# Seven block products in place of eight for the in-projection of a second MoE, in groups of two weight tiles

## The chip, the cores and the metric

One core of a Trainium2 chip. The metric is the device time of one execution in microseconds (us); before: median 705.96 of 3 runs (705.52 to 706.01). Engines are named TensorE (PE; its weight loads PEld), VectorE (DVE), ScalarE (ACT), GpSimd (POOL) and SyncE (SP, which issues DMAs here).

## What is computed

Three stages in sequence, in fp32 from float64 inputs (two 32-bit words per value): bucketed attention, a first MoE, a second MoE. B = 2, H = 8, S = 768, D = 64, so 1536 tokens of 512 values.

```python
scores = where(q_bucket == k_bucket, (q @ k.T) / sqrt(D), -1e9)
x = softmax(scores) @ v                                  # 1536 x 512
h = maximum(maximum(x @ w1, x @ w2), x @ w3)             # 512 -> 768
x = h @ w_out                                            # 768 -> 512
h = x @ m2_in                                            # 512 -> 2048
g = h / (1 + exp(-1.702 * h))
out = g @ m2_out                                         # 2048 -> 512
```

## The kernel before

Precision: TensorE multiplies in fp32r. Every operand is held as a high part (a copy rounded to fp32r, by ScalarE) and a low part (value minus high part, by GpSimd or VectorE), and every product is three matmuls: high x high, high x low, low x high.

Attention (L307 to L403): for each head and each 128 queries, `scores` (L307) makes a 128x768 tile in PSUM by four matmuls of 384 columns (two halves of the keys, each in its own bank, two contraction pieces), `clamp` (L319) brings it to SBUF with a minimum on VectorE, then Exp on ScalarE, scaling on GpSimd, transposes on TensorE (L346), the split into high and low (L352, L356) and the product with v (L364). A planner (`plan`, L47) with costs and due times (`COST`, `DUE`) fixes the order of all these tasks.

First MoE: `up1` (L554) for 6 feature tiles x 3 matrices x 3 token chunks of 512 (12 matmuls each, L561), `split1` (L576), `down1` (L584; 18 matmuls each, L594), whose result is X[1], the second MoE's input, as high and low parts `xh`, `xl` (128 x 4 x 1536).

Second MoE: 16 feature tiles (FT2) in 4 groups of 4 (FG = 4). `up2(f, a)` (L605) takes the 128 features f of chunk a: 4 contraction blocks x 3 matmuls = 12 matmuls of 512 columns (L612) into one PSUM bank, then sigmoid on ScalarE (L620), product on VectorE (L621), high part gh on ScalarE (L622), low part gl on GpSimd (L623). `down2(k, t)` (L625) takes 128 tokens: 4 tiles x 3 matmuls (L633) into one bank; group 0 copies it to `res` (L639, ScalarE), later groups add it (L641, VectorE), the last one stores it (L644). The loop at L870 runs the ups of one group and chunk, then the downs of the chunk before it.

Weights: each 128x512 block comes raw by DMA (512 KB; `w_load`, L436, two buffers WRAW) and is turned into fp32 by `w_steps` (L449): Abs on ScalarE (L456), clamp on GpSimd (L460), three VectorE steps of shift (L468), low word (L472) and sign (L476), after which the raw buffer is free and the next load is issued, then high part on ScalarE (L483) and low part on GpSimd (L496). Split tiles lie in rings of 6 ("w" for in-projections, "wo" for out-projections; WBUFS).

Order: each engine runs its instructions in the order of the program (`in_order`, L647). In the MoEs `unit` (L846) issues one up or down and then calls `w_tick` (L510), which moves each weight block in flight on by one step; a new block starts when enough matmuls have been issued (PACE, `owed`), at most three at once, and a block's split waits (and all behind it) until a buffer of its ring is free by program order (`w_free`, L504). PSUM in the MoEs is a ring of 8 banks (`bank`, L547).

Of the kernel before, what the change touches and what calls it, by code (L numbers as in the profile page):

```python
# [5 lines left out]
F32 = mybir.dt.float32  # L6
# [7 lines left out]
P = 128  # L14
# [76 lines left out]
def build(tc, q, k, v, proj, w1, w2, w3, w_out, m2_in, m2_out, out):  # L91
# [41 lines left out]

    def f32(ap):
        return ap.bitcast(F32)

    def halves(ap):
        return ap.rearrange("p (a n) -> p a n", a=2)

    def psum_halves(ap):  # L140
        return ap.rearrange("p (a n) -> p a n", a=2)[:, :, :HALF]


    warm = st([P, 512], "warm", 1, BF16)
# [162 lines left out]
    def scores(u):  # L307
        hd, c = divmod(u, NTILE)
        ks, qs = stacks[hd]
        pss = ps_s()  # L310
        for a in range(2):
            nc.tensor.matmul(pss[:, a * 512:a * 512 + HALF], qs[:, 0, c * P:(c + 1) * P],  # L312
                             ks[:, 0, a * HALF:(a + 1) * HALF], start=True, stop=False)
        for a in range(2):
            nc.tensor.matmul(pss[:, a * 512:a * 512 + HALF], qs[:D + NA, 1, c * P:(c + 1) * P],  # L315
                             ks[:D + NA, 1, a * HALF:(a + 1) * HALF], start=False, stop=True)
# [108 lines left out]
    for n in range(FT2 // FG):  # L425
        for f in range(n * FG, (n + 1) * FG):
            w_block(("in", f), m2_in[:, f * P:(f + 1) * P].rearrange("(c p) f -> p c f", p=P), EC, "w")
        if n > 0:
            w_out_group(n)
    WIDE = w1.dtype == U64  # L430
    WRAW = 2
    WBUFS = {"w": 6, "wo": 6}
    wraw, wsplit = {}, {}
    wstate = [0, 0]

    def w_load():  # L436
        i = wstate[0]
# [64 lines left out]
    wflight = []  # L502

    def w_free(i):  # L504

# [1 line left out]
        mine = [j for j in range(i) if wblocks[j][2] == tag]  # L507
        return len(mine) < WBUFS[tag] or mine[-WBUFS[tag]] in wdone

    def w_tick(start):  # L510
# [9 lines left out]
        if start and i < len(wblocks) and len(wflight) < 3 and (mo[0] is not None or wblocks[i][2] == "w"):  # L520
# [28 lines left out]
        return mo[1].tile([P, CH], F32, tag="acc", name=f"acc_{seq[0]}", bufs=8)  # L549

    def hm_tile():
        return st([P, CH], "hm", 4, pool=mo[0]) if mo[0] else st([P, CH], "hm0", 1)

    def up1(ft, i, a, get, later=False):  # L554
        wh, wl = w_get("up", ft, i)
# [49 lines left out]
    def up2(f, a):  # L605
        xh, xl = X[1]
        wh, wl = w_get("in", f)
        s = slice(a * CH, (a + 1) * CH)
        o = bank()
        for c in range(EC):  # L610
            for z, (w, x) in enumerate(((wh, xh), (wh, xl), (wl, xh))):
                nc.tensor.matmul(o, w[:, c, :], x[:, c, s], start=(c == 0 and z == 0),  # L612
                                 stop=(c == EC - 1 and z == 2))
        if a == NCH - 1:
            wdone.add(wplace["in", f])
        gh = st([P, CH], "gh", 2 * FG + 1, F32R, mo[2])
        gl = st([P, CH], "gl", 2 * FG + 1, F32R, mo[2])
        gs[f, a] = (gh, gl)
        g = hm_tile()
        nc.scalar.activation(g, o, AF.Sigmoid, scale=1.702)  # L620
        nc.vector.tensor_tensor(out=g, in0=o, in1=g, op=ALU.mult)  # L621
        nc.scalar.copy(gh, g)  # L622
        nc.gpsimd.tensor_tensor(out=gl, in0=g, in1=f32(gh), op=ALU.subtract)  # L623

    def down2(k, t):  # L625
        a, j = divmod(t, CH // P)
        s = slice(j * P, (j + 1) * P)
        ws = [w_get("out", k * FG + n) for n in range(FG)]
        o = bank()
        for n in range(FG):  # L630
            (gh, gl), (wh, wl) = gs[k * FG + n, a], ws[n]
            for z, (g, w) in enumerate(((gh, wh), (gh, wl), (gl, wh))):
                nc.tensor.matmul(o, g[:, s], w.rearrange("p c f -> p (c f)"),  # L633
                                 start=(n == 0 and z == 0), stop=(n == FG - 1 and z == 2))
        if t == B * NTILE - 1:
            wdone.update(wplace["out", k * FG + n] for n in range(FG))
        if k == 0:
            res[t] = st([P, E], "res", B * NTILE, F32, mo[2])
            nc.scalar.copy(res[t], o)  # L639
        else:  # L640
            nc.vector.tensor_tensor(out=res[t], in0=o, in1=res[t], op=ALU.add)  # L641
        if k == FT2 // FG - 1:
            b, c = divmod(t, NTILE)
            nc.sync.dma_start(out[b * S:(b + 1) * S, :].rearrange("(p c) e -> c p e", c=NTILE)[c], res[t])  # L644


    def in_order(first):  # L647
# [8 lines left out]
    if True:  # L656
# [186 lines left out]
        split1(0, 0)  # L843
        owed = [2 * PACE]

        def unit(fn, *args, after=None, matmuls=12):  # L846
            fn(*args)
            if after:
                after()
            owed[0] = min(owed[0] + matmuls / 12, 2 * PACE)  # L850
            for _ in range(1 if matmuls == 12 else 2):
                if w_tick(owed[0] >= PACE):
                    owed[0] -= PACE

        for a in range(1, NCH):
# [12 lines left out]
        NK = FT2 // FG  # L868
        ups = [(m, a) for m in range(NK) for a in range(NCH)]
        for n in range(len(ups) + 2):  # L870
            if n < len(ups):
                m, a = ups[n]
                for f in range(m * FG, (m + 1) * FG):
                    unit(up2, f, a)
            if n > 0 and n - 1 < len(ups):
                m, a = ups[n - 1]
                for t in range(a * CH // P, (a + 1) * CH // P):
                    unit(down2, m, t)
        in_order(first)
        sb_g.__exit__(None, None, None)  # L880
        ps_toe.__exit__(None, None, None)
# [31 lines left out]
```

## Time and profile before

| | us |
|---|---|
| median of 3 runs | 705.96 (705.52 to 706.01) |
| the profiled execution | 706.35 |
| its span, first to last instruction | 704.5 |
| attention, up to the first MoE's matmuls in one run | 0 to 251.2 |
| first MoE | 251.2 to 438.9 |
| second MoE | 438.9 to 704.5 |

In the table the stages are told by the first and last matmul of their lines. Rows of the trace give an engine, a line of the kernel, an operation with the tiles it writes and reads, and times in us unless ns is said. Matmul records overlap, as matmuls are pipelined, so the time of one is read from a block's length and count, not from its record.

### The profile page before, as it was taken

To read this page: it belongs to the slowest core of one execution; us is meant where nothing else is said; L and a number is where in the kernel's file an instruction comes from. 1 tells how busy PE (TensorE), PEld (TensorE's weight loads), DVE (VectorE), ACT (ScalarE), POOL (GpSimd) and SP (SyncE) were. 2 spreads that over 40 slices of the span, in tenths; PEclk is the share of its full clock that TensorE was granted. 3 is DMA by queue.
4 is the path that set the end of the run, shared out by engine and by line. 5 is a ranking of instruction groups with operands and counts; after the bars stand their busy time and mean duration, and the time that the engine had idled before them with its cause. 6 is when DMAs were issued, how large, how long until landed. Compare 5 with 4: busy or idle time off the path is not lost.

```text
span 704.5 us, 10764 instructions
## 1 busy us (share of the span) xinstructions
PE 696.7 (99%) x3777; PEld 602.9 (86%) x3778; DVE 449.8 (64%) x810; ACT 355.5 (50%) x698; POOL 389.7 (55%) x442
## 2 busy tenths in 40 slices
PE   8999999999999999999999999999999999999997
PEld 4899999999999988888888888888888888888886
DVE  7999999999999735764676354414435545554222
ACT  4898898888888713333342224444342333333220
POOL 5487878788888834643663423335454544453420
PEclk9999999999999999999999999999999999999999
DMA  5657676777554103332232132202122122120112
GB/s 112 143 128 158 131 182 144 172 181 158 115 135 98 49 5 111 98 112 68 90 90 67 53 92 88 61 0 60 60 60 60 60 60 60 60 91 0 46 45 90
DMA packets 74261, 63.34 MB, mean 90 GB/s; under 512 B 41360, under 2 KB 64912, under 8 KB 74208
## 3 DMA queue, kind: packets, MB, share of 16 engines
q1 hardware_dynamic: 74128, 62.65, 34.2%
q8 instruction: 30, 0.49, 0.3%
q14 instruction: 23, 0.19, 0.1%
q10 hardware_dynamic: 80, 0.00, 0.0%
HBM read 38.80 MB, written 3.15 MB: 60 GB/s over the span
## 4 chain that ended last, share of the span: by engine, by line
PE 78%; DVE 6%; issue 5%; POOL 4%; DMA 4%; ACT 1%; SPq 0%; POOLq 0%; ACTq 0%; DVEq 0%
PE acc L561 20%; PE acc L633 11%; PE acc L612 10%; PE PV L364 9%; PE T L346 8%; PE acc L594 7%; PE S L312 4%; PE S L315 4%; POOL gl L623 3%; DMA wraw<-in_moe_w_out_dram 2%; PE T L211 2%; PE T L184 1%; DVE wmag L476 1%; PE T L561 1%; DVE ptl L356 1%
## 5 line engine op out<-in xcount | busy, mean ns | idle before, releaser
L623 POOL TENSOR_TENSOR gl<-hm,gh 128x512 fp32r<-128x512 f32 x48 | 63.8, 1328 | 122.5 <-ACT gh L622 122.5
L456 ACT ACTIVATE wbits<-wraw 128x512 f32<-128x512 f32 (+1 forms) x58 | 37.8, 653 | 138.3 <-DMA wraw<-in_moe_w_out_dram 57.9
L337 POOL TENSOR_SCALAR se<-se,rc 128x768 f32<-128x768 f32 x96 | 86.7, 915 | 24.9 <-DVE rc L334 10.6
L621 DVE TENSOR_TENSOR hm<-acc,hm 128x512 f32<-128x512 f32 x48 | 33.1, 690 | 103.7 <-ACT hm L620 103.7
L356 DVE TENSOR_TENSOR ptl<-T,pth 128x512 fp32r<-128x512 f32 x144 | 94.5, 682 | 3.6 <-ACT pth L352 3.3
L329 ACT ACTIVATE se<-se,mn 128x768 f32<-128x768 f32 x96 | 90.8, 946 | 6.8 <-DVE se L323 6.0
L323 DVE TENSOR_SCALAR_CACHE_REDUCE se<-S 128x768 f32<-128x768 f32 x96 | 90.9, 949 | 1.7 <-PE S L315 1.3
L352 ACT CAST pth<-T 128x512 fp32r<-128x512 f32 x144 | 80.0, 588 | 12.3 <-PE T L346 10.3
L346 PE MATMUL T<-ident,se 128*128 128x128 f32 x576 | 80.3, 273 | 0.8 <-DVE ptl L356 0.5
L561 PE MATMUL acc<-xh,whi 128*128 128x512 f32 x204 | 79.4, 389 | 0.0
L561 PE MATMUL acc<-xl,whi 128*128 128x512 f32 x204 | 79.4, 389 | 0.0
L561 PE MATMUL acc<-xh,wlo 128*128 128x512 f32 x204 | 79.4, 389 | 0.0
L633 PE MATMUL acc<-wolo,gh 128*128 128x512 f32 x192 | 74.9, 390 | 0.2
L496 POOL TENSOR_TENSOR wlo<-wmag,whi 128x512 fp32r<-128x512 f32 (+1 forms) x42 | 55.9, 1330 | 34.3 <-ACT whi L483 34.3
L633 PE MATMUL acc<-wohi,gl 128*128 128x512 f32 x192 | 74.7, 389 | 0.0
L633 PE MATMUL acc<-wohi,gh 128*128 128x512 f32 x192 | 74.7, 389 | 0.0
L612 PE MATMUL acc<-xh,whi 128*128 128x512 f32 x192 | 74.7, 389 | 0.0
L612 PE MATMUL acc<-xl,whi 128*128 128x512 f32 x192 | 74.7, 389 | 0.0
L612 PE MATMUL acc<-xh,wlo 128*128 128x512 f32 x192 | 74.7, 389 | 0.0
L364 PE MATMUL PV<-pth,vst 128*128 128x256 f32 x288 | 74.6, 293 | 0.0
L346 PEld LDWEIGHTS T<-ident,se 128*128 128x128 f32 x576 | 66.6, 140 | 5.3 <-DVE ptl L356 1.1
L364 PE MATMUL PV<-ptl,vst 128*128 128x256 f32 x288 | 70.3, 279 | 0.0
(121 smaller groups left out, 1468.5 us busy)
## 6 DMA issues: line engine op xcount, KB each, us to landing
wraw<-in_moe_w_dram SPq DMA_DIRECT2D x18, 512.0 KB
wraw<-in_moe_w_out_dram SPq DMA_DIRECT2D x16, 512.0 KB
wraw<-in_moe_w_in_dram SPq DMA_DIRECT2D x16, 512.0 KB
kst<-kq SPq DMA_DIRECT2D x42, 192.0 KB
qst<-kq SPq DMA_DIRECT2D x42, 192.0 KB
raw<-in_k_dram SPq DMA_DIRECT2D x16, 192.0 KB
raw<-in_q_dram SPq DMA_DIRECT2D x16, 192.0 KB
raw<-in_v_dram SPq DMA_DIRECT2D x16, 192.0 KB
```

Source lines behind the costliest of these rows:

```text
L323: nc.vector.tensor_scalar(out=halves(se[u]), in0=psum_halves(pss), scalar1=1.0e9, scalar2=None, op0=ALU.min, op1=ALU.min, accum_out=mn[u])
L329: nc.scalar.activation(se[u], se[u], AF.Exp, bias=mn[u], scale=-1.0, accum_out=sm[u // 2][:, u % 2:u % 2 + 1])
L337: nc.gpsimd.tensor_scalar(out=se[u], in0=se[u], scalar1=rc[u // 2][:, u % 2:u % 2 + 1], scalar2=1.0, op0=ALU.mult, op1=ALU.mult)
L346: nc.tensor.transpose(pst[:, i * P:(i + 1) * P], se[2 * jq + o][:, c * P:(c + 1) * P], ident)
L352: nc.scalar.copy(ptr[jq][0][:, n * 512:(n + 1) * 512], tps[jq, n])
L356: nc.vector.tensor_tensor(out=ptr[jq][1][:, s], in0=tps[jq, n], in1=f32(ptr[jq][0][:, s]), op=ALU.subtract)
L364: nc.tensor.matmul(pv[jq], vs[:, c, :], ptr[jq][t].rearrange("p (o c n) -> p c o n", o=2, c=NTILE)[:, c], start=(c == 0 and t == 0), stop= ...
L496: nc.gpsimd.tensor_tensor(out=lo[:, :n], in0=t, in1=f32(hi[:, :n]), op=ALU.subtract)
L561: nc.tensor.matmul(o, w[:, c, :], x[:, c, s], start=(c == 0 and z == 0), stop=(c == EC - 1 and z == 2))
L612: nc.tensor.matmul(o, w[:, c, :], x[:, c, s], start=(c == 0 and z == 0), stop=(c == EC - 1 and z == 2))
L623: nc.gpsimd.tensor_tensor(out=gl, in0=g, in1=f32(gh), op=ALU.subtract)
L633: nc.tensor.matmul(o, g[:, s], w.rearrange("p c f -> p (c f)"), start=(n == 0 and z == 0), stop=(n == FG - 1 and z == 2))
```

## The change

In the second MoE the groups become two tiles (FG = 2; 8 groups). Group 0 runs `up2` as before, all its chunks first and then its 12 downs. In groups 1 to 7 the two tiles by token chunks 0 and 1 are four output blocks, with the contraction in two halves; `seven` makes them by Strassen's seven block products (Winograd's form, with sums S1 to S4 of weight blocks and T1 to T4 of token blocks), 6 matmuls each; chunk 2 still goes through `up2`. A product's result is combined with the earlier ones on VectorE into SBUF tiles, from which sigmoid and product read. `token_sums` makes T1 to T4 once, during group 0; `sum_steps` makes S1 to S4 for each later pair, as further steps in the queue of weights. `down2` takes 6 matmuls per 128 tokens and adds to `res` in every group after 0; the very last block goes in two halves of 256 columns, stored by two queues. Weight blocks have a finer step list in this stage, each unit names how many must have been started (`target`), up to five are in flight, and the order of blocks is out-projections before the in-projections of their group. Rings: "w" and "wo" 6 to 4, `wmag` 2 to 4, `hm` 4 to 3, `hm0` 1 to 2, gh and gl 9 to 6. In the attention the scores are two matmuls of 512 and two of 256 columns in one run of 768, which `clamp` reads as one run.

```diff
-        for a in range(2):
-            nc.tensor.matmul(pss[:, a * 512:a * 512 + HALF], qs[:, 0, c * P:(c + 1) * P],
-                             ks[:, 0, a * HALF:(a + 1) * HALF], start=True, stop=False)
...
+        for x, k in ((slice(0, 512), 0), (slice(512, S), 0), (slice(0, 512), 1), (slice(512, S), 1)):
+            r = slice(0, D + NA if k else P)
+            nc.tensor.matmul(pss[:, x], qs[r, k, c * P:(c + 1) * P], ks[r, k, x], start=k == 0, stop=k == 1)
...
-        nc.vector.tensor_scalar(out=halves(se[u]), in0=psum_halves(pss), scalar1=1.0e9, scalar2=None,
+        nc.vector.tensor_scalar(out=se[u], in0=pss[:, :S], scalar1=1.0e9, scalar2=None,
...
-    FG = 4
+    FG = 2
...
-    WBUFS = {"w": 6, "wo": 6}
+    WBUFS = {"w": 4, "wo": 4}
...
+        def whole():
+            sign()
+            w_load()
+            wf[i] = f32(got["w"])
+            if i in wpair:
+                wflight.append((None, sum_steps(wpair[i])))
...
+        if WIDE and wstage[0]:
+            return [magnitude, clamp, lambda: None, shift, low, whole, split, lower]
...
+    def sum_steps(p):
+        a1, a2 = (wf[wplace["in", 2 * p + n]] for n in range(2))
+        got = {}
+        def first():
+            got["x"] = st([P, 2, 2, P], "hm0", 2)
+            s1, s2 = (got["x"][:, n] for n in range(2))
+            nc.gpsimd.tensor_tensor(out=s1, in0=a2[:, 0:2], in1=a2[:, 2:4], op=ALU.add)
+            nc.gpsimd.tensor_tensor(out=s2, in0=s1, in1=a1[:, 0:2], op=ALU.subtract)
+        def second():
+            got["y"] = st([P, 2, 2, P], "hm0", 2)
+            s3, s4 = (got["y"][:, n] for n in range(2))
+            nc.gpsimd.tensor_tensor(out=s3, in0=a1[:, 0:2], in1=a2[:, 0:2], op=ALU.subtract)
+            nc.gpsimd.tensor_tensor(out=s4, in0=a1[:, 2:4], in1=got["x"][:, 1], op=ALU.subtract)
+        def high():
+            got["s"] = st([P, 4, 2, P], "shi", 1, F32R, mo[2]), st([P, 4, 2, P], "slo", 1, F32R, mo[2])
+            for n, t in enumerate("xy"):
+                nc.scalar.copy(got["s"][0][:, 2 * n:2 * n + 2], got[t])
+        def low():
+            for n, t in enumerate("xy"):
+                r = slice(2 * n, 2 * n + 2)
+                nc.gpsimd.tensor_tensor(out=got["s"][1][:, r], in0=got[t], in1=f32(got["s"][0][:, r]), op=ALU.subtract)
+            sums[p] = got["s"]
+        return [first, second, high, low]
...
-            if len(steps) == 2 and not w_free(i):
+            if i is not None and len(steps) == 2 and not w_free(i) or i is None and not sums_free():
                 break
...
+    def gelu(f, a, h):
+        gs[f, a] = tuple(st([P, CH], tag, 6, F32R, mo[2]) for tag in ("gh", "gl"))
+        gh, gl = gs[f, a]
+        g = hm_tile()
+        nc.scalar.activation(g, h, AF.Sigmoid, scale=1.702)
+        def rest():
+            nc.vector.tensor_tensor(out=g, in0=h, in1=g, op=ALU.mult)
+            nc.scalar.copy(gh, g)
+            nc.gpsimd.tensor_tensor(out=gl, in0=g, in1=f32(gh), op=ALU.subtract)
+        return rest
...
+        def p1(o):
+            held["u"] = st([P, CH], "hc", 4, pool=mo[0])
+            nc.scalar.copy(held["u"], o)
+        def p2(o):
+            held["c11"] = st([P, CH], "hc", 4, pool=mo[0])
+            add(held["c11"], o, held["u"])
+            return gelu(f, 0, held["c11"])
+        def p6(o):
+            add(held["u"], o, held["u"])
+        def p7(o):
+            held["v"] = st([P, CH], "hc", 4, pool=mo[0])
+            add(held["v"], o, held["u"])
+        def p5(o):
+            held["c22"] = st([P, CH], "hc", 4, pool=mo[0])
+            add(held["c22"], o, held["v"])
+            nc.vector.tensor_tensor(out=held["v"], in0=held["v"], in1=held["p4"], op=ALU.subtract)
+            rest = gelu(f + 1, 0, held["v"]), gelu(f + 1, 1, held["c22"])
+            add(held["u"], o, held["u"])
+            return lambda: [x() for x in rest]
+        def p4(o):
+            held["p4"] = o
+        def p3(o):
+            add(held["u"], o, held["u"])
+            return gelu(f, 1, held["u"])
...
+                turns = [(w, x, c) for c in range(2) for w, x in ((wh, xh), (wh, xl))] + [(wl, xh, c) for c in range(2)]
...
+                rest = then(o)
+                while due:
+                    due.pop(0)()
+                if rest:
+                    due.append(rest)
...
+        return [product(*x) for x in (("11", "11", p1), ("12", "21", p2), ("22", "T4", p4), ("S2", "T2", p6),
+                                      ("S3", "T3", p7), ("S1", "T1", p5), ("S4", "22", p3))], due
...
+            turns = [(gs[k * FG + n, a][0], w) for n in range(FG) for w in ws[n]]
+            turns += [(gs[k * FG + n, a][1], ws[n][0]) for n in range(FG)]
...
+        for p in range(FT2 // FG):
+            nxt = wplace["in", FG * p + FG - 1] + 1
+            if p == 0:
+                for n in range(NCH * FG):
+                    unit(up2, n % FG, n // FG, after=ahead, target=nxt + 1 + (n >= 1) + (n >= 3) + (n >= 4))
+                    w_tick(False)
+            else:
...
+                products, due = seven(p)
+                for n, x in enumerate(products):
+                    unit(x, matmuls=6, target=nxt + 1 + (n >= 3) + (n >= 6))
+                for f in range(FG):
+                    unit(up2, FG * p + f, NCH - 1, after=lambda: due and due.pop(0)(), target=nxt + 3)
+            for t in range(B * NTILE):
+                unit(down2, p, t, matmuls=6, after=ahead, target=nxt + 4)
```

`token_sums` is ten short steps that `ahead` issues one per unit in group 0: for each of two contraction blocks four additions of high and low part, four differences (VectorE), four high parts (ScalarE) and four low parts (two on VectorE, two on GpSimd), all 128x512.

## Rows read from the trace of the kernel before

**Rows 1.** The page: busy us of each engine with its share of the span and its count of instructions, and the TensorE clock granted in 40 slices, in tenths.
```profile
PE 696.7 (99%) x3777; PEld 602.9 (86%) x3778; DVE 449.8 (64%) x810; ACT 355.5 (50%) x698; POOL 389.7 (55%) x442
PEclk9999999999999999999999999999999999999999
```

**Rows 2.** The chain that ended last, in order of time: start, length in us, engine, tile, line and count.
```profile
251.21 138.72 PE acc L561 x612
...
438.89 21.76 PE acc L612 x96
460.65 10.88 PE acc L633 x48
...
679.11 21.77 PE acc L633 x96
...
700.90 0.69 DVE res L641
```

**Rows 3.** Busy time by stretch (the attention, the second MoE, and a quarter of the latter): the stretch, its length, then PE, PEld, DVE, ACT and POOL busy us with counts, the granted clock, DMA share and GB/s.
```profile
40.00:230.00 190.00, 189.04 (x1436) 183.66 (x1435) 183.68 (x410) 165.14 (x354) 157.41 (x207) 1.00 0.64 146
438.89:701.00 262.11, 261.75 (x1152) 215.71 (x1151) 110.61 (x154) 89.19 (x155) 111.01 (x94) 1.00 0.17 54
...
591.00:656.00 65.00, 64.89 (x286) 53.40 (x285) 32.13 (x46) 22.74 (x40) 34.06 (x29) 1.00 0.16 49
```

**Rows 4.** VectorE lines, whole span: count, then ns of one as least/median/most, first and last start, shapes.
```profile
L468 DVE TENSOR_SCALAR wmag<-wbits x58: 345/423/1531, 117.4 to 647.1; 128x512 uint32<-128x512 uint32 x50, 128x384 uint32<-128x384 uint32 x8
L472 DVE SCALAR_TENSOR_TENSOR wmag<-wraw,wmag x58: 557/693/1802, 125.7 to 647.6; 128x512 uint32<-128x512 uint32 x50, 128x384 uint32<-128x384 uint32 x8
L476 DVE SCALAR_TENSOR_TENSOR wmag<-wraw,wmag x58: 557/720/1671, 137.5 to 648.3; 128x512 uint32<-128x512 uint32 x50, 128x384 uint32<-128x384 uint32 x8
L621 DVE TENSOR_TENSOR hm<-acc,hm x48: 678/691/692, 449.7 to 679.8; 128x512 f32<-128x512 f32 x48
L641 DVE TENSOR_TENSOR res<-acc,res x36: 674/680/692, 541.3 to 700.9; 128x512 f32<-128x512 f32 x36
```

**Rows 5.** GpSimd lines, the same columns.
```profile
L460 POOL TENSOR_SCALAR wbits<-wbits x58: 507/614/1130, 114.5 to 633.5; 128x512 f32<-128x512 f32 x50, 128x384 f32<-128x384 f32 x8
L496 POOL TENSOR_TENSOR wolo<-wmag,wohi x16: 1273/1292/1742, 346.2 to 655.3; 128x512 fp32r<-128x512 f32 x16
L623 POOL TENSOR_TENSOR gl<-hm,gh x48: 1285/1294/1587, 451.1 to 681.3; 128x512 fp32r<-128x512 f32 x48
L403 POOL TENSOR_TENSOR xl<-xf,xh x24: 729/736/1054, 49.0 to 249.5; 128x256 fp32r<-128x256 f32 x24
```

**Rows 6.** ScalarE lines, the same columns.
```profile
L456 ACT ACTIVATE wbits<-wraw x58: 548/666/711, 113.5 to 632.8; 128x512 f32<-128x512 f32 x50, 128x384 f32<-128x384 f32 x8
L483 ACT CAST wohi<-wmag x16: 604/616/624, 344.6 to 651.2; 128x512 fp32r<-128x512 f32 x16
L620 ACT ACTIVATE hm<-acc x48: 572/591/613, 449.0 to 679.2; 128x512 f32<-128x512 f32 x48
L622 ACT CAST gh<-hm x48: 619/621/625, 450.4 to 680.6; 128x512 fp32r<-128x512 f32 x48
```

**Rows 7.** The timeline from 512.8 us of VectorE and GpSimd: start, length in us, engine, line, operation.
```profile
512.89 0.69 DVE L472 SCALAR_TENSOR_TENSOR wmag<-wraw,wmag 128x512 uint32<-128x512 uint32 x1
513.15 1.59 POOL L623 TENSOR_TENSOR gl<-hm,gh 128x512 fp32r<-128x512 f32 x1 [0.58 <-ACT gh L622]
513.62 1.67 DVE L476 SCALAR_TENSOR_TENSOR wmag<-wraw,wmag 128x512 uint32<-128x512 uint32 x1
514.70 1.06 POOL L460 TENSOR_SCALAR wbits<-wbits 128x512 f32<-128x512 f32 x1
```

**Rows 8.** Groups of instructions from 591.2 to 656.4 us: count, busy us and mean ns of one, then the idle time before them.
```profile
L476 DVE SCALAR_TENSOR_TENSOR wmag<-wraw,wmag 128x512 uint32<-128x512 uint32 x7 | 8.7, 1248 | 0.2
L472 DVE SCALAR_TENSOR_TENSOR wmag<-wraw,wmag 128x512 uint32<-128x512 uint32 x7 | 4.8, 692 | 0.2
L468 DVE TENSOR_SCALAR wmag<-wbits 128x512 uint32<-128x512 uint32 x7 | 2.9, 420 | 4.5 <-POOL wlo L496 3.3 <-POOL wbits L460 1.2
```

**Rows 9.** The chain that ended last, three waits for raw weights in the second MoE: start, length, what.
```profile
482.72 3.20 DMA wraw<-in_moe_w_out_dram
...
497.39 3.35 DMA wraw<-in_moe_w_out_dram
...
532.96 3.70 DMA wraw<-in_moe_w_in_dram
```

**Rows 10.** The chain that ended last, two blocks in the attention: of 256 columns (the product with v) and of 384 (the bucket bits).
```profile
157.02 0.70 PE PV L364 x6
...
167.01 1.05 PE T L211 x6
```

**Rows 11.** VectorE lines that read PSUM, of 384, 512 and 768 columns; columns as in rows 4.
```profile
L199 DVE TENSOR_TENSOR kq<-T,kq x14: 544/552/557, 19.3 to 193.6; 128x384 fp32r<-128x384 f32 x14
L356 DVE TENSOR_TENSOR ptl<-T,pth x144: 669/681/693, 25.5 to 241.1; 128x512 fp32r<-128x512 f32 x144
L323 DVE TENSOR_SCALAR_CACHE_REDUCE se<-S x96: 937/948/960, 12.8 to 234.0; 128x768 f32<-128x768 f32 x96
```

More of the change, by code (lines that the diff above doesn't have):

```diff
@@ L499, in w_steps @@
             return [magnitude, clamp, shift, low, sign, split, lower]
+        if WIDE and wstage[0]:
+            return [magnitude, clamp, lambda: None, shift, low, whole, split, lower]
         return ([magnitude, clamp, bits] if WIDE else []) + [split, lower]
     wflight = []
+    wpair = {wplace["in", 2 * p + 1]: p for p in range(1, FT2 // 2)}
     def w_free(i):
@@ L508, in w_free, with sums_free @@
         return len(mine) < WBUFS[tag] or mine[-WBUFS[tag]] in wdone
+    def sums_free():
+        return len(sums) == len(sdone)
+    def sum_steps(p):
[21 more added lines that the diff above has]
+        return [first, second, high, low]
+    sums, sdone = {}, set()
     def w_tick(start):
@@ L519, in w_tick @@
         i = wstate[1]
-        if start and i < len(wblocks) and len(wflight) < 3 and (mo[0] is not None or wblocks[i][2] == "w"):
+        if start and i < len(wblocks) and len(wflight) < (5 if wstage[0] else 3) and i in wraw and (mo[0] is not None or wblocks[i][2] == "w"):
             wflight.append((i, w_steps(i)))
@@ L615, in up2 @@
             wdone.add(wplace["in", f])
[L616 to L618 removed]
+        gelu(f, a, o)()
+    def gelu(f, a, h):
+        gs[f, a] = tuple(st([P, CH], tag, 6, F32R, mo[2]) for tag in ("gh", "gl"))
+        gh, gl = gs[f, a]
         g = hm_tile()
[L620 to L622 removed]
@@ L623, in up2, with token_sums, block, split @@
-        nc.gpsimd.tensor_tensor(out=gl, in0=g, in1=f32(gh), op=ALU.subtract)
+        nc.scalar.activation(g, h, AF.Sigmoid, scale=1.702)
[4 more added lines that the diff above has]
+        return rest
+    ts = {}
+    def token_sums():
+        xh, xl = X[1]
+        steps = []
+        for n in range(4):
+            ts[n] = tuple(st([P, 2, CH], f"t{z}{n}", 1, F32R, mo[2]) for z in "hl")
+        def block(c, half, a):
+            t = st([P, CH], "hc", 4, pool=mo[0])
+            s = slice(a * CH, (a + 1) * CH)
+            nc.vector.tensor_tensor(out=t, in0=f32(xh[:, c + 2 * half, s]), in1=f32(xl[:, c + 2 * half, s]), op=ALU.add)
+            return t
+        def split(n, c, t, eng):
+            nc.scalar.copy(ts[n][0][:, c], t)
+            eng.tensor_tensor(out=ts[n][1][:, c], in0=t, in1=f32(ts[n][0][:, c]), op=ALU.subtract)
+        for c in range(2):
+            got = {}
+            def one(c=c, got=got):
+                got["11"], got["12"] = block(c, 0, 0), block(c, 0, 1)
+                nc.vector.tensor_tensor(out=got["11"], in0=got["12"], in1=got["11"], op=ALU.subtract)
+            def two(c=c, got=got):
+                split(0, c, got["11"], nc.gpsimd)
+                got["22"] = block(c, 1, 1)
+                nc.vector.tensor_tensor(out=got["12"], in0=got["22"], in1=got["12"], op=ALU.subtract)
+            def three(c=c, got=got):
+                split(2, c, got["12"], nc.vector)
+                nc.vector.tensor_tensor(out=got["22"], in0=got["22"], in1=got["11"], op=ALU.subtract)
+                got["21"] = block(c, 1, 0)
+            def four(c=c, got=got):
+                split(1, c, got["22"], nc.gpsimd)
+                nc.vector.tensor_tensor(out=got["21"], in0=got["22"], in1=got["21"], op=ALU.subtract)
+            def five(c=c, got=got):
+                split(3, c, got["21"], nc.vector)
+            steps += [one, two, three, four, five]
+        return steps
@@ new lines, in seven, with add, product, run @@
+    def seven(p):
+        f = 2 * p
+        (ah, al), (bh, bl) = w_get("in", f), w_get("in", f + 1)
+        xh, xl = X[1]
+        sh, sl = sums[p]
+        A = {"11": (ah[:, 0:2], al[:, 0:2]), "12": (ah[:, 2:4], al[:, 2:4]), "22": (bh[:, 2:4], bl[:, 2:4])}
+        A.update((f"S{n + 1}", (sh[:, n], sl[:, n])) for n in range(4))
+        B = {f"{c + 1}{a + 1}": tuple(x[:, 2 * c:2 * c + 2, a * CH:(a + 1) * CH] for x in (xh, xl))
+             for c in range(2) for a in range(2)}
+        B.update((f"T{n + 1}", ts[n]) for n in range(4))
+        due = []
+        held = {}
+        def add(to, o, with_):
+            nc.vector.tensor_tensor(out=to, in0=o, in1=with_, op=ALU.add)
+        def p1(o):
[22 more added lines that the diff above has]
+            return gelu(f, 1, held["u"])
+        def product(left, right, then):
+            def run():
+                o = bank()
+                (wh, wl), (xh, xl) = A[left], B[right]
+                turns = [(w, x, c) for c in range(2) for w, x in ((wh, xh), (wh, xl))] + [(wl, xh, c) for c in range(2)]
+                for n, (w, x, c) in enumerate(turns):
+                    nc.tensor.matmul(o, w[:, c], x[:, c], start=n == 0, stop=n == len(turns) - 1)
+                if then is p3:
+                    sdone.add(p)
+                rest = then(o)
[3 more added lines that the diff above has]
+                    due.append(rest)
+            return run
+        return [product(*x) for x in (("11", "11", p1), ("12", "21", p2), ("22", "T4", p4), ("S2", "T2", p6),
+                                      ("S3", "T3", p7), ("S1", "T1", p5), ("S4", "22", p3))], due
@@ L628, in down2 @@
         ws = [w_get("out", k * FG + n) for n in range(FG)]
[L629 to L634, printed above, removed]
+        ends = k == FT2 // FG - 1
+        b, c = divmod(t, NTILE)
+        to = out[b * S:(b + 1) * S, :].rearrange("(p c) e -> c p e", c=NTILE)[c]
+        halves = 2 if ends and t == B * NTILE - 1 else 1
+        for e in (slice(i * E // halves, (i + 1) * E // halves) for i in range(halves)):
+            o = bank()[:, :E // halves]
+            turns = [(gs[k * FG + n, a][0], w) for n in range(FG) for w in ws[n]]
+            turns += [(gs[k * FG + n, a][1], ws[n][0]) for n in range(FG)]
+            for n, (g, w) in enumerate(turns):
+                nc.tensor.matmul(o, g[:, s], w.rearrange("p c f -> p (c f)")[:, e], start=n == 0, stop=n == len(turns) - 1)
+            if k == 0:
+                res[t] = st([P, E], "res", B * NTILE, F32, mo[2])
+                nc.scalar.copy(res[t], o)
+            else:
+                nc.vector.tensor_tensor(out=res[t][:, e], in0=o, in1=res[t][:, e], op=ALU.add)
+            if ends:
+                (nc.sync if e.start == 0 else nc.scalar).dma_start(to[:, e], res[t][:, e])
         if t == B * NTILE - 1:
             wdone.update(wplace["out", k * FG + n] for n in range(FG))
[L637 to L644, printed above, removed]
     def in_order(first):
@@ L844, in build, with unit @@
         owed = [2 * PACE]
-        def unit(fn, *args, after=None, matmuls=12):
+        def unit(fn, *args, after=None, matmuls=12, target=None):
             fn(*args)
@@ L849, in unit @@
                 after()
+            if target is not None:
+                w_tick(wstate[1] < target)
+                return
             owed[0] = min(owed[0] + matmuls / 12, 2 * PACE)
-            for _ in range(1 if matmuls == 12 else 2):
-                if w_tick(owed[0] >= PACE):
+            for _ in range(2 if matmuls > 12 else 1):
+                if w_tick(owed[0] >= PACE and wstate[1] < wplace["in", FG]):
                     owed[0] -= PACE
@@ L867, in build, with ahead @@
         mo[2] = sb_g.__enter__()
[L868 to L878, printed above, removed]
+        steps = token_sums()
+        wstage[0] = True
+        def ahead():
+            if steps:
+                steps.pop(0)()
+        for p in range(FT2 // FG):
[4 more added lines that the diff above has]
+                    w_tick(False)
+            else:
+                while steps:
+                    steps.pop(0)()
+                products, due = seven(p)
[5 more added lines that the diff above has]
+                unit(down2, p, t, matmuls=6, after=ahead, target=nxt + 4)
         in_order(first)
```

18 lines of the change are left out of this document (6 added, 12 removed).

## The prediction

> **What bounds the kernel now.** I read the page's busy lines first, then the chain that ended last, then busy time by stretch, then the durations by line. The page shows TensorE busy 99% at a granted clock of nine tenths or more in every slice [rows 1]; that alone proves little, since matmul records overlap, so the chain must confirm it. It does: from 251 us to the end it runs through matmuls in blocks, 612 in 138.72 us, 96 in 21.76, 48 in 10.88, so one 512-column matmul costs 0.2267 us, wherever it stands [rows 2]. The second MoE (438.89 to 700.88) holds 1152 of them: 261.1 of its 262.0 us. It is bound by TensorE's count of matmuls. Beside it VectorE is busy 110.6, GpSimd 111.0 and ScalarE 89.2 of 262 us [rows 3]: they have room now, and the change spends it. In the attention (40 to 230 us) TensorE is busy 189.04 and VectorE 183.68 of 190 us: both near full [rows 3].
>
> **What the change removes.** Let a group be two weight tiles of w_in, with their two of w_out. For groups 1 to 7 the two tiles by chunks 0 and 1 took 4 x 12 = 48 matmuls; seven products take 7 x 6 = 42. 7 x 6 = 42 matmuls go: 42 x 0.2267 = **-9.52 us**. Group 0 stays at 144 matmuls (32.6 us); each later group is 42 + 24 + 72 = 138, or 31.28 us. That these matmuls go is counted from the code; whether the others still follow without gaps is the question.
>
> **What it adds, per group of 31.28 us** (undelayed durations [rows 4, 5, 6]).
> VectorE: four weight tiles at 0.42 + 0.69 + 0.69 = 1.80 each, 7.2; six sigmoid products, 4.1; seven additions that recombine the products, 7 x 0.69 = 4.8; twelve additions into the result, 8.2 (they now come for every two tiles, not every four). 24.3 us.
> GpSimd: four clamps 2.4, four low parts 5.2, six gl 7.7, four half-size weight sums at 0.74 (priced by the 128x256 subtraction) 3.0, two low parts of sums 2.6. 20.9 us.
> ScalarE: 4 x 0.67 + 4 x 0.62 + 6 x (0.59 + 0.62) + 0.59 + 2 x 0.62 = 14.2 us.
> So each still fits beside TensorE, VectorE at 78%, but no longer with ease: waits inside the queues decide.
>
> **First wait, between VectorE and GpSimd.** VectorE operations with two SBUF inputs stretch when GpSimd runs: the low-word step goes from 0.69 to 1.80 at most, the sign step to 1.67, while the sigmoid product with one input in PSUM never leaves 0.678 to 0.692 [rows 4]. One place shows how: the sign step starts at 513.62 beside a gl that runs to 514.74, and takes 1.67 instead of 0.69; the clamp behind that gl takes 1.06 instead of 0.61 [rows 7]. Only one of the two sides moves at a time. Between 591 and 656 us this costs a tile 1.248 - 0.693 = 0.555 us, with GpSimd busy 34.06 of 65 us [rows 3, 8]. After the change GpSimd is busy 67% instead of 52%, and four of the six sigmoid products read an SBUF copy instead of PSUM, so 16 VectorE operations per group are exposed. I take 0.22 us each (0.555 / 3, raised by 67/52): 3.6 us, VectorE 27.9.
> How long one side holds the other: the four operations from 512.89 to the end of the clamp at 515.76 take 2.87 us, though undelayed they sum to 0.69 + 1.29 + 0.69 + 0.61 = 3.28 [rows 4, 5, 7]: a factor 0.87, since starts and ends overlap. Exposed work in a group is 7.2 + 4 x 0.69 + 20.9 = 30.9 us; by 0.87 it is 26.9 of 31.28. The Trainium skill, "SBUF — State Buffer", section "SBUF: two separate sides", says that the shared pair of ports is an exclusive lock held for the whole instruction, the other side fully blocked. By that the pair would be needed 30.9 of 31.28 us and the sum would be that of the first rival below; the row speaks for the milder reading.
>
> **Second wait, the raw weights.** With two raw buffers the load for a group's third tile starts at the sign step of its first, and ScalarE's Abs for it is issued one unit later. Landing takes 3.2 to 3.7 us [rows 9], the Abs 0.67; behind it on ScalarE stands the sigmoid of the chunk-2 tile (0.59), and VectorE's product of it heads VectorE's queue. That is 4.6 us, in which VectorE has one addition, two products and a shift, 2.5 us. So VectorE idles about 2.1 us per group, however late it runs. VectorE's loop: 27.9 + 2.1 = 30.0, under 31.28.
>
> **Third, three meeting points on TensorE.** Time from the group's first product. (a) The sixth product (P5 in the code's names) ends at 8.16; two additions (1.4), sigmoid (0.59; meanwhile VectorE's next addition, the sign step and P3's addition, 2.1), product, high part, gl (0.69, 0.62, 1.30 [rows 4 to 6]) end near 14.6. The first output block starts at 14.96 and needs gl at its fifth matmul, 15.87: 1.3 us to spare. (b) The weight sums of the next group: from the first tile's sign step (11.1) to the last tile's, VectorE has 13.6 us of work, the 2.1 us idle and some 2.6 of stretching: 29.4. Then on GpSimd two sums, the tile's low part, two sums, the first low part: 1.5 + 1.3 + 1.5 + 1.3, 35.0. The fourth product needs it at 31.28 + 4.99 = 36.3: 1.3 us to spare. (c) PSUM: eight banks of at least 1.36 us each, so an addition into the result may be late by several us free of charge. One stretch of 0.98 fits in (a) or (b), two overshoot by 0.66; with two in every second group the cost is 0.33 x 6 = **+2.0 us**. Bounds: 0, and 8 (1.3 us in each of the six groups that prepare weights).
>
> **Group 0** adds the token sums: 20 VectorE operations (13.8 us), 21.5 in all beside 32.6; GpSimd 22.2. Exposed work 17.4 + 22.2 = 39.6, by 0.87 34.5, against a limit of 32.6 + 2.7 (first use of a token sum): covered. Group 7 prepares no weights.
>
> **Small edits.** Scores: four matmuls of 384 columns become two of 512 and two of 256. The nearest rows give 1.05 / 6 = 0.175 and 0.70 / 6 = 0.117 us [rows 10]: 4 x 0.175 = 0.700 against 0.687, 96 times -1.2 us if TensorE alone set the pace, 0 if VectorE does: **-0.6**, ends -1.2 and +0.5. The clamp reads 768 columns in one run: 384 columns take 0.552, 512 take 0.681 [rows 11], which extended gives 0.94, against 0.948 now: nothing. Tail: the last block in two halves costs 12 x 0.117 - 6 x 0.2267 = +0.04; its last addition shrinks from 0.69 [rows 2] to about 0.42 by that slope, -0.27. The last store, 704.5 - 701.6 = 2.9 us now, carries half the bytes on another queue: -0.1, ends -0.6 and +0.4. Four buffers of w tiles instead of six: in the first MoE a tile is split once the fourth before it is done, is ready two units later, and is used nine units (24 us of matmuls) after; nothing, unless that cover is gone. Three "hm" buffers instead of four: five us of matmuls between the last reader's start and the next writer, and PSUM behind it; nothing.
>
> **Sum.** The profiled execution took 706.35 us (span 704.5 and 1.85 around it); the median is 0.39 lower. 706.35 - 9.52 + 0.04 - 0.27 - 0.1 - 0.6 + 2.0 = 697.9; less 0.39, **697.5 us**. Without waits 695.5.
>
> **Rivals.** 0.2% (1.4 us) is about what can be told from no change.
> Rival 1, no change: VectorE and GpSimd exclude each other for whole instructions. Then 30.9 us of exposed work and the 2.1 us idle make 33.0 per group, 1.7 over, in six groups 10: 705.6. For it: the stretches to 1.67. Against: 2.87 for 3.28.
> Rival 2, slower: VectorE's queue. If each of the 16 exposed operations meets the 0.555 us that a tile's sign step meets now, 8.9 us, VectorE needs 24.3 + 8.9 + 0.4 of the idle time that this leaves = 33.6, 2.3 over in six groups, 14: 709.5. It decides from about 33.0 per group, where six overruns eat 9.9. For it: GpSimd is busier and the sign step already starts beside a gl at a fixed place in the order. Against: the shift and low-word steps show 0.42 and 0.69, undelayed, in the same stretch [rows 8].
> Rival 3, no waits at all: 695.5 or less, if stretches fall where TensorE has its 1.3 us.
>
> **Chances.** Forecast (696 to 701) 0.62; rival 3 0.13; half eaten (701 to 704.5) 0.08; rival 1 0.06; rival 2 0.11. Faster 0.83, same 0.06, slower 0.11. The range reaches from 694.5 (no wait, and the small edits at their better ends) to 704.0 (waits of 8 us).
>
> **What would show it.** Right: seven products in blocks of 0.2267 us, 534 matmuls on the in-projection's lines instead of 576, VectorE 75 to 90% busy in the second MoE, TensorE idle under 0.7 us per group, and that ahead of the products that use sums or the first output block. Wrong: gaps of over 1.5 us in each group with VectorE as releaser (rival 2), or with GpSimd's low parts (rival 1); a longer attention.

## The result, and the profile after

| | us | ratio to before (95% interval) |
|---|---|---|
| before | 705.99 (705.52 to 706.67, 4 runs) | |
| changed | 712.92 (712.69 to 713.66, 4 runs) | 1.0099 (1.0082 to 1.0117) |

The change makes the kernel slower by 6.9 us. The profiled span grew from 704.5 to 710.9. The page after, busy time of each engine:

```profile
PE 694.3 (98%) x3741; PEld 590.9 (83%) x3742; DVE 525.4 (74%) x928; ACT 373.7 (53%) x727; POOL 438.0 (62%) x488
```

VectorE has 76 us more work than before [rows 1], TensorE hardly less, although it issues fewer matmuls. Busy time by stretch, columns as in [rows 3]: group 0, most of group 1, then 33 us from the later groups:

```profile
437.00:474.00 37.00, 34.58 (x146) 27.76 (x145) 30.04 (x35) 17.82 (x31) 21.26 (x16) 0.95 0.12 37
474.00:507.00 33.00, 30.21 (x125) 24.27 (x125) 19.65 (x27) 16.53 (x31) 20.40 (x19) 0.95 0.13 39
...
540.00:573.00 33.00, 31.95 (x140) 25.81 (x139) 25.73 (x38) 13.62 (x24) 22.21 (x20) 1.00 0.21 65
```

TensorE, which had no gaps there before [rows 2], now has them in every stretch. What it waited for in the second MoE (us in total, times, longest):

```profile
PE acc L769 <- POOL slo L541: 4.4, 6, 0.8
...
PE acc L769 <- ACT res L798: 2.8, 1, 2.8
...
PE acc L795 <- ACT res L798: 2.4, 2, 2.0
...
PE acc L795 <- POOL gl L665: 1.2, 5, 0.3
```

L769 are the seven products, L541 the low parts of the weight sums, L798 the copies of group 0 into `res`, L795 the output blocks. Two separate losses stand behind these lines, a late start (L798) and a long cycle (L541, L665).

**The account.** Before, the second MoE's matmuls ran from 438.73 to 700.88, 262.15 us, of which 1152 x 0.2267 = 261.2 are matmuls. Now they run from 437.77 to 707.74, 269.97 us, of which 1104 x 0.2267 + 12 x 0.117 = 251.7 are. So 9.5 us of matmuls went, as counted, and the time beyond them grew from 1.0 to 18.3. Nine of these are the start: group 1's fourth product, due at 437.77 + 32.64 + 4.08 = 474.49, began at 483.64. The other nine are the cycle: the weight sums (L524) for groups 2 to 7 begin at 510.83, 543.71, 576.70, ..., 675.57, every 32.95 us instead of 31.28; that is five turns of 1.67 us, and 0.6 at group 2's fourth product.

### The long cycle, followed back

The chain that ended last, from the last weight tile's sign step in one group to the products of the next:

```profile
543.03 0.61 DVE wmag L468
...
543.71 0.75 POOL hm L524
544.53 0.74 POOL hm L525
...
546.48 0.74 POOL hm L530
547.22 0.70 POOL hm L531
547.92 1.25 POOL slo L541
...
549.21 4.83 PE acc L769 x20
```

TensorE's fourth product stands until a low part is done at 549.17. Meanwhile ScalarE and VectorE, at the same place (the timelines):

```profile
547.95 0.62 ACT L536 CAST shi<-hm 128x512 fp32r<-128x512 f32 x1 [2.03 <-POOL hm L531]
548.48 0.58 ACT L734 COPY hc<-acc 128x512 f32<-128x512 f32 x1
```
```profile
549.09 0.69 DVE L730 TENSOR_TENSOR hc<-acc,hc 128x512 f32<-128x512 f32 x1 [1.86 <-ACT hc L734]
```

ScalarE waits 2.03 us for the second pair of sums; the first product's evacuation (L734), long ready, stands behind that copy, and VectorE's first addition waits 1.86 us for the evacuation. VectorE starts the group late, its weight steps are late, and so are the next sums: a loop in which TensorE has no part. VectorE's instructions over one turn of it (549.09 to 582.07; columns as in [rows 8]). L460, L464 and L468 are the shift, low-word and sign steps (L468, L472, L476 in [rows 4, 8]), L663 the sigmoid products (L621), L800 the additions into `res` (L641), L730 and L751 the recombinations:

```profile
L800 DVE TENSOR_TENSOR res<-acc,res 128x512 f32<-128x512 f32 x12 | 7.7, 679 | 0.0
L464 DVE SCALAR_TENSOR_TENSOR wmag<-wraw,wmag 128x512 uint32<-128x512 uint32 x4 | 4.2, 1058 | 0.0
L730 DVE TENSOR_TENSOR hc<-acc,hc 128x512 f32<-128x512 f32 x6 | 4.1, 683 | 1.9 <-ACT hc L734 1.9
L468 DVE SCALAR_TENSOR_TENSOR wmag<-wraw,wmag 128x512 uint32<-128x512 uint32 x4 | 3.8, 951 | 0.0
L663 DVE TENSOR_TENSOR hm<-hc,hm 128x512 f32<-128x512 f32 x4 | 3.0, 776 | 0.7 <-ACT hm L660 0.7
L460 DVE TENSOR_SCALAR wmag<-wbits 128x512 uint32<-128x512 uint32 x4 | 2.8, 688 | 1.2 <-POOL wbits L452 1.2
L663 DVE TENSOR_TENSOR hm<-acc,hm 128x512 f32<-128x512 f32 x2 | 1.4, 692 | 3.5 <-ACT hm L660 3.5
L751 DVE TENSOR_TENSOR hc<-hc,acc 128x512 f32<-128x512 f32 x1 | 0.7, 690 | 0.0
```

Count times mean sums to 28.2 us; back to back the records overlap (an addition of 0.68 starts every 0.60), so 25.7 us of the turn is busy time (as in the stretch from 540 above) and 1.9 + 0.7 + 1.2 + 3.5 = 7.3 us is waiting. 25.7 + 7.3 = 33.0: VectorE is not full, it stands in a queue of short waits. None of them is for TensorE.

### The late start

ScalarE in group 0 (its timeline; L686 are copies of token sums, L798 the evacuations of output blocks into `res`):

```profile
461.17 0.58 ACT L798 COPY res<-acc 128x512 f32<-128x512 f32 x1
463.55 0.63 ACT L686 CAST th<-hc 128x512 fp32r<-128x512 f32 x1 [1.79 <-DVE hc L694]
...
465.40 0.58 ACT L798 COPY res<-acc 128x512 f32<-128x512 f32 x1
468.74 0.62 ACT L686 CAST th<-hc 128x512 fp32r<-128x512 f32 x1 [2.76 <-DVE hc L699]
469.26 0.58 ACT L798 COPY res<-acc 128x512 f32<-128x512 f32 x1
...
478.07 0.62 ACT L536 CAST shi<-hm 128x512 fp32r<-128x512 f32 x1 [2.43 <-POOL hm L531]
478.60 3.51 ACT L798 COPY res<-acc 128x512 f32<-128x512 f32 x7
```

Blocks end every 1.36 us on TensorE, but each copy into `res` stands behind a token copy that waits for VectorE: 4.2 and 3.9 us apart. The last seven stand behind a copy of a weight sum and run together from 478.60. TensorE waits for the banks that these copies free. Granted clock (last number but two) and TensorE's busy time in stretches of 2 us:

```profile
468.00:470.00 2.00, 0.10 (x1) 0.11 (x1) 1.91 (x3) 1.10 (x2) 0.00 (x0) 1.00 0.00 0
470.00:472.00 2.00, 2.00 (x5) 1.61 (x6) 2.00 (x5) 0.69 (x2) 0.59 (x1) 0.51 0.00 0
...
476.00:478.00 2.00, 0.44 (x2) 0.01 (x1) 0.00 (x0) 0.00 (x0) 2.00 (x3) 1.00 0.00 0
...
480.00:482.00 2.00, 2.00 (x7) 1.53 (x6) 0.00 (x0) 2.00 (x6) 0.52 (x1) 0.57 0.00 0
```

After TensorE had stood for most of 2 us, the granted clock was at about half, 1.2 GHz, in the next stretch, and again (0.57) after the stop that begins near 476. Matmuls there start every 0.43 us instead of 0.23; some 3 of the nine us are that. Such stops do not always bring it: in the profiled execution with a third raw buffer (below) TensorE stood at the same three blocks, 5.5 us together, the granted clock stayed at 1.00, and the fourth product was 6.7 us late.

### The profile page after: what moved, and what is told of

It reads as the page before. It is cut to its first block, busy times and chain, and to the rows that moved or that the text cites. A ratio compares the mean times of both kernels' runs of the same rounds, so it can differ in the third digit from the quotient of the medians.

```text
span 710.9 us, 10936 instructions
## 1 busy us (share of the span) xinstructions
PE 694.3 (98%) x3741; PEld 590.9 (83%) x3742; DVE 525.4 (74%) x928; ACT 373.7 (53%) x727; POOL 438.0 (62%) x488
## 3 DMA queue, kind: packets, MB, share of 16 engines
q1 hardware_dynamic: 74128, 62.52, 33.8%
## 4 chain that ended last, share of the span: by engine, by line
PE 66%; DVE 13%; POOL 9%; issue 7%; ACT 3%; DMA 1%; SPq 0%; POOLq 0%; DVEq 0%; ACTq 0%
PE acc L598 20%; PE S L307 9%; PE PV L355 8%; PE T L337 8%; PE acc L631 5%; PE acc L795 5%; PE acc L649 3%; PE acc L769 3%; DVE res L800 3%; POOL gl L665 2%; DVE wmag L464 2%; PE T L205 2%; POOL wolo L495 1%; PE T L178 1%; PE T L598 1%
## 5 line engine op out<-in xcount | busy, mean ns | idle before, releaser
L665 POOL TENSOR_TENSOR gl<-hm,gh 128x512 fp32r<-128x512 f32 x48 | 65.6, 1379 | 59.1 <-ACT gh L664 59.1
L307 PE MATMUL S<-kst,qst 128*128 128x512 f32 (+3 forms) x384 | 87.1, 350 | 0.0
L598 PE MATMUL acc<-xh,whi 128*128 128x512 f32 x204 | 79.4, 389 | 0.0
L598 PE MATMUL acc<-xl,whi 128*128 128x512 f32 x204 | 79.4, 389 | 0.0
L598 PE MATMUL acc<-xh,wlo 128*128 128x512 f32 x204 | 79.4, 389 | 0.0
L795 PE MATMUL acc<-wohi,gh 128*128 128x512 f32 (+1 forms) x194 | 75.8, 391 | 2.4 <-ACT res L798 2.4
L795 PE MATMUL acc<-wolo,gh 128*128 128x512 f32 (+1 forms) x194 | 75.5, 390 | 0.0
L495 POOL TENSOR_TENSOR wlo<-wmag,whi 128x512 fp32r<-128x512 f32 (+1 forms) x42 | 53.7, 1278 | 33.8 <-ACT whi L475 33.7
L452 POOL TENSOR_SCALAR wbits<-wbits 128x512 f32<-128x512 f32 (+1 forms) x58 | 41.0, 707 | 42.5 <-ACT wbits L448 42.1
L608 DVE TENSOR_TENSOR hm<-acc,hm 128x512 f32<-128x512 f32 x34 | 23.5, 691 | 56.9 <-PE acc L598 54.5
L307 PEld LDWEIGHTS S<-kst,qst 76*128 76x128 f32 (+1 forms) x384 | 59.2, 190 | 5.2 <-DVE se L314 0.5
L795 PE MATMUL acc<-wohi,gl 128*128 128x512 f32 (+1 forms) x194 | 60.4, 392 | 1.2 <-POOL gl L665 1.2
```

The source lines that it names most:

```text
L307: nc.tensor.matmul(pss[:, x], qs[r, k, c * P:(c + 1) * P], ks[r, k, x], start=k == 0, stop=k == 1)
```

## Experiments

Theory: the two losses are loops and waits in the order of the queues, and go when the order or a buffer is changed, with the same work. Rival: VectorE and GpSimd have too much to do beside each other (they exclude each other, or are full), whatever the order. Each edit is against the changed kernel unless another is named; "cycle" is the time from one group's weight sums to the next group's, 32.95 us in the changed kernel.

**The scores alone**, in the kernel before (the two hunks of `scores` and `clamp`).

> The kernel before with the new scores and clamp alone. The changed kernel reaches its first run of 612 matmuls 0.96 us earlier (250.25 against 251.21), so 1.0 us less than before: 705.0. Rival: the 0.96 us come from another edit that moved buffers; then 706.0.

706.18 us, ratio 1.0005 (0.9995 to 1.0014): nothing to be seen. The first MoE's run of matmuls starts at 250.82 here, and at 250.25 to 251.13 in kernels with the same attention: the 0.96 us lie within what one profile differs from the next.

**Groups of two without products.**

```diff
-        steps = token_sums()
+        steps = []
...
-            if p == 0:
+            if True:
```

> The changed kernel without the seven products (every group as group 0: six ups, twelve downs; no token sums, no weight sums); 1152 matmuls again. If the additions, sums and their order cost the time, TensorE runs without gaps: 706.0 - 1.0 (scores) - 0.4 (tail) = 704.6. If groups of two themselves cost (twice the additions into the result, finer weight steps, smaller rings), it is above 706, up to 713.

704.62, ratio 0.9981 (0.9972 to 0.9990), as expected. TensorE is busy all of the second MoE:

```profile
437.00:700.00 263.00, 263.00 (x1166) 217.82 (x1165) 151.90 (x215) 96.97 (x163) 126.39 (x103) 1.00 0.19 60
```

The finer groups, smaller rings and halved last block cost nothing; what the seven products add must carry the loss.

**w_in tiles ahead of w_out tiles.**

```diff
-        if n > 0:
+        if n == 1:
             w_out_group(n)
...
+        if n > 1:
+            w_out_group(n)
...
-            nxt = wplace["in", FG * p + FG - 1] + 1
+            nxt = wplace["in", 0] + FG + 2 * FG * p
```

> The changed kernel with one order turned: from group 2's weights on, a group's two w_in tiles are prepared ahead of its two w_out tiles. Same work on every engine. Theory (a loop through the queues: the weight sums come last in a group, ScalarE's copy of the second pair of sums stands ahead of the first product's evacuation, so VectorE starts each group late and the sums come late again): the cycle of 33.0 us per group falls to 31.3 to 31.6, six groups give 8 to 10 us: 703 to 705. Rival (VectorE and GpSimd are over capacity by exclusion, 33.0 per group whatever the order): 712 to 714.

717.58, ratio 1.0164 (1.0149 to 1.0179): a miss of 13 us. The sums did come earlier, but the group's last tile now had its clamp behind them on GpSimd, and its high part on ScalarE took the sums' place ahead of the evacuation:

```profile
577.08 1.50 DVE L462 TENSOR_SCALAR wmag<-wbits 128x512 uint32<-128x512 uint32 x1 [2.56 <-POOL wbits L454]
```
```profile
581.98 0.62 ACT L477 CAST wohi<-wmag 128x512 fp32r<-128x512 f32 x1 [4.35 <-DVE wmag L470]
582.51 0.58 ACT L736 COPY hc<-acc 128x512 f32<-128x512 f32 x1
```

The cycle is 33.8 us. My claim that the sums' place closes the loop was wrong: another late copy ahead of the evacuation does it too. The same work in another order moved the cycle, so the order counts; but the cycle only grew, and a lower limit at 33.0 is not excluded by this run.

**Token sums left out.**

```diff
-        B.update((f"T{n + 1}", ts[n]) for n in range(4))
+        B.update((f"T{n + 1}", B[x]) for n, x in enumerate(("11", "12", "21", "22")))
...
-        steps = token_sums()
+        steps = []
```

> The changed kernel with the token sums left out (token blocks in their place, so 20 VectorE, 8 ScalarE and 4 GpSimd operations of group 0 go). Theory: group 1's fourth product started 9.0 us late (483.2 instead of 437.5 + 32.6 + 4.1 = 474.2), nearly all by the token sums in group 0: 712.9 - 8 = 705, groups 1 to 6 still 33.0 us. Rival: the late start is from the weight sums of the first pair or the clock; then 711 to 713.

703.86, ratio 0.9964 (0.9950 to 0.9978): 9.1 us less than the changed kernel, the nine of the account, lower clock included (here it is 1.00); the cycle stays at 33.0 (sums at 535.18, 568.12, 601.03).

**A third raw buffer.**

```diff
-    WRAW = 2
+    WRAW = 3
...
         wstage[0] = True
+        w_load()
```

> The changed kernel with a third raw weight buffer, its load issued one block earlier through the second MoE (room for it: wmag ring 3, hc ring 3 with c22 in c11's tile). Theory (a loop in which each group's third tile waits for its raw load, 3.8 us from the first tile's sign step to ScalarE's Abs, with the chunk-2 sigmoid and VectorE behind it): VectorE's idle 2.9 us per group there falls under 1, the cycle from 33.0 to 31.3 to 31.6, six groups: 702.5 to 705. Rival (exclusion of VectorE and GpSimd sets 33.0): 711 to 714.

706.64, ratio 1.0014 (1.0003 to 1.0025): 6.3 us less, cycle 32.0, less gained than expected. The shorter cycle gives some 5 of the 6.3; the rest lies in the late start, where the clock did not fall in the profiled execution. VectorE's wait for the chunk-2 sigmoid only fell to 1.92, since ScalarE does other things first:

```profile
588.19 0.61 ACT L475 CAST wohi<-wmag 128x512 fp32r<-128x512 f32 x1
588.71 0.66 ACT L448 ACTIVATE wbits<-wraw 128x512 f32<-128x512 f32 x1
589.28 0.57 ACT L660 ACTIVATE hm<-acc 128x512 f32<-128x512 f32 x1
```

One of the 2.9 us was the raw load; the rest is ScalarE's order.

**Evacuation of the first product by VectorE.**

```diff
-            nc.scalar.copy(held["u"], o)
+            nc.vector.tensor_copy(held["u"], o)
```

> The changed kernel with the first product of each group copied out of PSUM by VectorE instead of ScalarE. Theory (ScalarE's copy of the second pair of sums, waiting for GpSimd, stands ahead of that evacuation and is a link of the loop): VectorE no longer idles 1.86 us there, but copies 0.6: the loop is 1.2 shorter, 31.8 per group, 705 to 706.5. Rival (the link is not on the loop; VectorE's own work sets 33.0): 0.6 more per group, 716.

709.12, ratio 1.0045 (1.0028 to 1.0062): 3.8 us less, cycle 32.35. The 1.86 us wait is gone (0.1 left), 0.6 came as work and the next sigmoid's wait grew from 0.7 to 1.1. The link is on the loop, at half the size expected. And with more work on VectorE the cycle fell, which it would not if VectorE were full.

**Token sums over groups 0 and 1**, products from group 2 on, a step in every third unit; then the same with the third raw buffer.

```diff
-            if steps:
+            calls[0] += 1
+            if steps and calls[0] % 3 == 0:
...
-            if p == 0:
+            if p < 2:
```

> The changed kernel with the seven products from group 2 on and the token sums spread over groups 0 and 1, one step in every third unit. Theory: the late start of 9 us goes, six more matmuls cost 1.4, and one group less runs the 33.0 us cycle (1.7): 712.9 - 9.0 + 1.4 - 1.7 = 703.6. If the start is late for another reason (the first pair's weight sums): 711 to 714.

> Both mended (third raw buffer, token sums over two groups). Theory: TensorE without waits of note, 36 matmuls fewer than before: 706.0 - 8.2 - 0.4 = 697.4, up to 699. Rival (exclusion): group cycle 33.0, 703 to 705.

710.97, ratio 1.0073 (1.0058 to 1.0088), and 705.37, ratio 0.9994 (0.9985 to 1.0004): misses of 7 to 8 us. The last token copy now stood behind the copy of a weight sum on ScalarE, its low part headed VectorE's queue, and six additions into `res` came after it (first of the two kernels):

```profile
508.75 0.62 ACT L536 CAST shi<-hm 128x512 fp32r<-128x512 f32 x1 [2.01 <-POOL hm L531]
509.28 0.61 ACT L686 CAST th<-hc 128x512 fp32r<-128x512 f32 x1
```
```profile
509.92 1.84 DVE L687 TENSOR_TENSOR tl<-hc,th 128x512 fp32r<-128x512 f32 x1 [2.64 <-ACT th L686]
511.69 3.67 DVE L800 TENSOR_TENSOR res<-acc,res 128x512 f32<-128x512 f32 x6
```

So the next run changed only the place: every second unit (`calls[0] % 2`), the last step in group 1's second unit.

> As the run with the token sums spread over groups 0 and 1 and products from group 2, but a step in every second unit, so that the last is issued in the second unit of group 1 and none stands behind the first pair's weight sums on ScalarE. Theory: no late start; 712.9 - 9.1 + 1.4 - 1.7 = 703.5, cycle still 33.0. Rival (VectorE has too much to do at that place whatever the order): 709 to 711 as with every third unit.

703.35, ratio 0.9965 (0.9952 to 0.9978), as expected, with the cycle still at 32.95; TensorE is busy 37.00 of 37 and 33.00 of 33 us where it had the late start.

**Third raw buffer, token sums left out.**

> Third raw buffer and token sums left out (token blocks in their place). If the two losses are separate they add: 712.9 - 9.1 (token sums, as measured) - 6.3 (raw buffer, as measured) = 697.5. If the late start and the long cycle share a cause, more: 700 to 704.

698.40, ratio 0.9895 (0.9880 to 0.9910), 0.8 from the sum of the two: separate losses.

**All that helped:** third raw buffer, token sums in every second unit with products from group 2, evacuation by VectorE.

> Third raw buffer, token sums in every second unit with products from group 2, and the first product copied out by VectorE. Theory: cycle 31.3 to 31.6 in six groups, no late start, 36 matmuls fewer than before: 697.5 to 699.5, faster than both kernels. Rival (exclusion keeps the cycle at 32.0, as with the third raw buffer alone): 701 to 703.

**696.96 us**, ratio 0.9872 (0.9856 to 0.9889): 9.0 us under the kernel before, 16.0 under the changed one, and 0.5 under the range expected. The chain that ended last is TensorE's alone, as in [rows 2]:

```profile
566.30 9.52 PE acc L769 x42
575.83 5.44 PE acc L649 x24
581.26 16.32 PE acc L795 x72
597.59 9.53 PE acc L769 x42
...
628.88 9.78 PE acc L769 x42
...
660.42 9.74 PE acc L769 x42
```

42 matmuls of the products, 24 of chunk 2 and 72 of the output blocks take 31.29 us, the ideal. Only the products of the last two groups take longer, 9.78 and 9.74 us: the weight sums still come every 31.5 us (533.78, 565.26, 596.76, 628.28, 659.77), so the loop through the queues is still 0.2 us longer than TensorE's turn and has caught up with it there. VectorE's exposed steps, over one turn (565.26 to 596.76), are stretched as much as in the changed kernel:

```profile
L464 DVE SCALAR_TENSOR_TENSOR wmag<-wraw,wmag 128x512 uint32<-128x512 uint32 x4 | 4.2, 1056 | 0.0
L468 DVE SCALAR_TENSOR_TENSOR wmag<-wraw,wmag 128x512 uint32<-128x512 uint32 x4 | 3.8, 950 | 0.0
```

## Why the prediction was wrong, step by step

- **Matmuls removed, 9.5 us: right.** The blocks of the last run, 31.29 us for 138 matmuls, show it.
- **VectorE's work, 27.9 us with stretches: right** (28.2 in records). The stretches were taken as 3.6 (16 x 0.22 is 3.5; 0.555 / 3 raised by 67/52 is 0.24, which gives 3.8); per turn L460, L464, L468 and the four SBUF products lie above their undelayed times by 4 x (0.27 + 0.37 + 0.26) + 4 x 0.09 = 3.9.
- **"So VectorE idles about 2.1 us per group": the step that failed.** It idles 7.3. The wait foreseen (chunk-2 sigmoid) was 2.9, and only 1.0 of it the raw load. Not foreseen: the evacuation behind the copy of the sums 1.9, the sigmoids after it and of the second chunk-2 tile 1.3 together, the clamp behind gl and a low part on GpSimd 1.2. The loop 27.9 + 2.1 = 30.0 became 28.2 + 7.3 = 35.5, less 2.5 us by which records overlap, 33.0.
- **Meeting point (b), 1.3 us to spare: fell with it.** The last sign step came near 33.4 us of the group instead of 29.4, the low part 1 us after its need instead of 1.3 before. (a) held for the first output block; the fifth waited 0.3 us for its gl (L665). (c) held for the additions of groups 1 to 7, for which TensorE never waited; the copies of group 0 broke it.
- **"Group 0 ... covered": the second failure, 9.1 us.** I added up VectorE and GpSimd and left out ScalarE's order, in which copies of token sums that wait stand ahead of the copies that free PSUM. Some 3 us of it are the lower clock behind the stops, for which the sum had no term.
- **The scores, -0.6:** not to be seen, 706.18 against 705.99. The four matmuls of a tile were to take 0.687 us instead of 0.700; on the chains near 228 us they take 0.70 in both traces. The tail was right in size: last addition 0.42, last store 2.7 us.
- **Rivals.** Rival 2 named the right engine and nearly the cycle (33.6), for the wrong reason: it had each exposed step stretched more, and they were not. Rival 1 gave 33.0, the cycle measured, also for the wrong reason: the exposed work is the same in the last kernel, whose cycle is 31.5. By the forecast's own sign, gaps ahead of GpSimd's low parts, the profile spoke for rival 1; but the low parts were late because VectorE's sign steps before them were, with GpSimd busy 22.2 of 33 us. Neither rival had the late start, so neither reached 712.9. The Trainium skill, "SBUF — State Buffer", section "SBUF: two separate sides", has the shared ports locked for the whole instruction. The trace agrees that one side waits (the stretches are there in every kernel); the sum of 30.9 us alone would still fit into 31.5, so the runs do not refute the rule, only that it set 33.0.
- **Open:** no run took the stretches away, so what a cycle without them would be is not shown.

## What to carry to other kernels

When a change adds work to engines beside a saturated one, their busy share says little: write out each in-order queue and ask of every instruction that can wait what stands behind it, above all evacuations that free PSUM or start the next group. A loop that runs through several queues without touching the bound engine sets its own cycle; it is found by following one turn back from the stall, and here it was cured by order, a buffer and another engine for one copy, with nearly the same work. A copy whose input is late should not stand ahead of those that are ready; moving one behind them on the same engine is not shown here, and the one order that was turned (w_in ahead of w_out) only put another late copy in its place.

## What the runs showed of the hardware

Records of VectorE overlap: additions of 0.68 us start every 0.60, so sums of records overstate its load by some 10% here (28.2 against 25.7). Stops of TensorE of 2.0 and 2.8 us were followed by a granted clock of 0.51 and 0.57 in the changed kernel, with matmuls every 0.43 us, and stops of 1.2, 1.5 and 2.8 us by 1.00 throughout in the run with a third raw buffer: the price of such a stop differs between these two profiled executions, and why is not shown.
